# Softmax in eleven parts with halo rows from the neighbour, input loads on GpSimd's queue, z blocks in turn, another order of the value products

## The chip, the cores and the metric

One core of a Trainium2 chip runs the kernel. The metric is device time in microseconds of one execution; the median of three runs before the change is 603.17 us (594.58 to 603.51).

## The reference, cut to what matters

Sizes: B = 8 batches, S = 4224 rows, D = 192 channels, H = 8 heads of 24 channels, K = 7 taps, all float32.

```python
w = exp(weight_gen - max(weight_gen, axis=-1))          # (B, S, H, 7)
w = w / (sum(w, axis=-1) + 1e-9)                        # softmax over the 7 taps
out[b,s,h,:] = sum over k of w[b,s,h,k] * x[b, s-6+k, h,:]   # rows before 0 are zero
gate = sigmoid(sum over j of conv_w[j] * out[b, s-4+j, :])   # 5 taps, per channel
y = (gate * (out @ w_val)) @ w_out                      # two 192x192 products
```

## The kernel before, in words

**Softmax and z.** The softmax of weight_gen is computed in 7 parts of 192 to 960 sequence rows of each batch (R = 12, 16, 28, 28, 60, 60, 60 rows in each of 128 partitions; partition 16l+q holds rows q*R to q*R+R of batch l's part). Each part also holds the 6 rows behind each partition's own (`PAD`), loaded and computed a second time, because a z row needs the weights of later rows. On DVE: `max`, `sub`, `sum`, `recip`, `norm`; on ACT: `exp` (L224 to L250). Four ACT copies (`spread`, L267) then put the weights of up to 12 rows into a zero-filled tile `zt` (two of them), so that each row of 184 numbers is a piece of a banded matrix, and `store` (L281) writes it to a DRAM block z. Blocks are new and get whole rows with their zeros (736 B per row); the last part reuses the block of the fifth and writes only the 72 numbers that change (288 B per row).

**Groups.** The sequence is cut into 36 groups (the first and last of 72 rows, the others of 120), each for all 8 batches. For group m, `load_x` (L299) brings its rows and 6 before them into one of three tiles `xt`; `load_t` (L322) reads the banded matrix back out of z in some 8 pieces of 16 rows into one of two tiles `tb`. `bank` (L335) then does the dynamic convolution as matmuls, four kinds into PSUM tiles `pa` (three buffers). ACT's `evac` (L354) takes kinds 0 and 1 to `ringA`, kind 2 to `ringB`, kind 3 to a tile `S`; twelve small transfers on POOL's queue (`move`, L362 and L364, four to ringB, then eight to ringA) place the pieces of S into holes of the rings. The gate of a group is one ACT product (`tap0`, L382) and four DVE multiply-adds (`tap`, L389) for each of A and B, then a sigmoid on ACT (L394). `val` (L404 to L412) is the product with w_val, `gv` (L418, L420) the gating, `omm` (L433, L440) the product with w_out, `oev` (L454) its copy to `ot`, and `store` (L461) two transfers to the output, twice per group.

**Order.** Every call is put in a list with a hand-written time (`at`, `stage`) and the list is sorted: the times fix only the order on each engine and queue; waits are put in by data dependence. Group m's stage begins at `when(m)` (13.05 apart): its bank and moves fall in that stage, its taps and `val` in the next, `omm` in the one after that. `load_x` and `load_t` of group m stand at `when(m-1)`. All of weight_gen's loads (one for each batch and half part), x, z, tb and output transfers are issued by SP in that order, but for four on ACT; POOL issues the moves and, at the start, the weights' transfers, and fills tiles and converts the weights.

Of the kernel before, what the change touches and what calls it, by code (L numbers as in the profile page):

```python
# [17 lines left out]
def tile_dynconv_gated_moe(  # L18
# [47 lines left out]
    ZQ = 4  # L66
# [21 lines left out]
    wf = const.tile([P, 2, NWT], FP32, name="wf")  # L88
    un = const.tile([P, 2, NWT], U32, name="un")
# [4 lines left out]
    cw = wf[:, :, 2 * D:]  # L94
    woa = wf[:, 0, D:2 * D]
    wob = wf[:, 1, D:2 * D]
# [29 lines left out]
    def convert_weights(cs, v, w):  # L126

        lo_w, hi_w = raw[:, :, cs, 0], raw[:, :, cs, 1]
        t = wf[:, :, cs].bitcast(U32)
        u = un[:, :, cs]  # L130
        tf, uf = wf[:, :, cs], u.bitcast(FP32)
# [16 lines left out]
    def place_weights():  # L148
# [9 lines left out]
        pairs = [*runs(wvm, wf[:, 0, 0:D], 4, NQ)]  # L158
        for b in range(2):
            hs = slice(HD * b, HD * b + HD)  # L160
            pairs += runs(wvd[hs, hs], wf[hs, 1, 0:D], 4, NQ)
        pairs += [*runs(wva, wf[:, 0, 0:D], 0, 4), *runs(wvb, wf[:, 1, 0:D], 0, 4)]
# [9 lines left out]

    class Block:


        def __init__(self, n, name):
            self.n, self.used = n, False
            self.t = dpool.tile([L, n, PITCH], FP32, name=name)

    blocks = [Block(16 * R, f"z{i}") for i, R in enumerate((12, 16, 28, 28, 60, 60))]  # L180
# [3 lines left out]
    class Softmax:  # L184

        ROWS = 60 + PAD

        def __init__(self, r0, R, block):
            self.r0, self.R, self.n = r0, R, R + PAD
            self.block, self.old = block, block.used  # L190
            block.used = True
            assert block.n == 16 * R
            h = -(-self.n // 22)
            self.cut = [(self.n * k // h, self.n * (k + 1) // h) for k in range(h)]
            self.zc = [(c, min(c + ZR, R)) for c in range(0, R, ZR)]
            where.append(r0)

        def tiles(self):
            self.wt = wpool.tile([P, self.ROWS, H, K], FP32, name="wt")[:, 0:self.n]
            self.mx = wpool.tile([P, self.ROWS, H], FP32, name="mx")[:, 0:self.n]  # L200
            if self.r0 + 16 * self.R == S:
                nc.vector.memset(self.wt[P - Q:P, self.R:], 0.0)

        def load(self, l, c0, c1, eng):


            R = self.R
            flat = self.wt.rearrange("p r h k -> p (r h k)")
            src = wg.offset + (l * S + self.r0) * ROW

            def part(q, c0, c1):
                if c0 < c1:
                    s = bass.AP(tensor=wg.tensor, offset=src + c0 * ROW, ap=[[R * ROW, q], [1, (c1 - c0) * ROW]])
                    eng.dma_start(out=flat[16 * l:16 * l + q, c0 * ROW:c1 * ROW], in_=s)

            if l == L - 1 and self.r0 + 16 * R == S:
                part(16, c0, min(c1, R))
                part(15, max(c0, R), c1)
            else:
                part(16, c0, c1)  # L220

        def max(self, k):
            a, b = self.cut[k]
            nc.vector.tensor_reduce(out=self.mx[:, a:b], in_=self.wt[:, a:b], axis=AX.X, op=ALU.max)  # L224

        def wide(self, k):
            a, b = self.cut[k]
            return self.wt[:, a:b], self.mx[:, a:b].unsqueeze(3).broadcast_to([P, b - a, H, K])

        def sub(self, k):  # L230
            w, m = self.wide(k)
            nc.vector.tensor_tensor(out=w, in0=w, in1=m, op=ALU.subtract)

        def exp(self, k):
            a, b = self.cut[k]
            nc.scalar.activation(out=self.wt[:, a:b], in_=self.wt[:, a:b], func=AF.Exp)

        def sum(self, k):
            a, b = self.cut[k]
            nc.vector.tensor_reduce(out=self.mx[:, a:b], in_=self.wt[:, a:b], axis=AX.X, op=ALU.add)  # L240

        def recip(self, k):
            a, b = self.cut[k]
            m = self.mx[:, a:b]
# [3 lines left out]
        def norm(self, k):  # L248
            w, m = self.wide(k)
            nc.vector.tensor_tensor(out=w, in0=w, in1=m, op=ALU.mult)  # L250

        def spread(self, c):
# [5 lines left out]
            for e in range(2):  # L258
                for o in range(2):
# [7 lines left out]
                    nc.scalar.copy(out=dst, in_=src)  # L267

        def store(self, c):


            a, b = self.zc[c]
            d0 = self.block.t[0, a, :]
            step, n = (PITCH, DATA) if self.old else (ZQ * PITCH, ZQ * PITCH)
            dst = bass.AP(tensor=d0.tensor, offset=d0.offset,
                          ap=[[self.R * PITCH, P], [step, (b - a) * PITCH // step], [1, n]])
            if self.old:
                src = self.z[:, 0:b - a, 0:DATA]
            else:
                src = self.z[:, 0:b - a].rearrange("p (r q) c -> p r (q c)", q=ZQ)  # L280
            nc.sync.dma_start(out=dst, in_=src)  # L281


    class Group:
# [400 lines left out]
```

## Time and profile before

| | us |
|---|---|
| median of 3 runs | 603.17 (594.58 to 603.51) |
| the profiled execution | 596.75, span 595.0 |
| busy: PE / DVE / ACT / POOL | 489.3 / 422.0 / 316.8 / 257.8 |
| mean granted TensorE clock | 0.925 |
| moved by DMA | 115.44 MB |

Busy time is that of instructions on the engine; matmuls are pipelined, so a busy PE isn't at its peak. The granted clock is 1.0 at 2.4 GHz and 0.5 at 1.2 GHz. The DMA share is the mean busy share of the 16 DMA engines. A wait is put down to what came last by the profile.

### The profile page before, as it was taken

The numbers are of one execution on the slowest core, as the hardware profiler recorded it, in microseconds if no ns is written. First come the engines' busy times: TensorE is split into PE (matmuls) and PEld (weight loads), VectorE is DVE, ScalarE is ACT, GpSimd is POOL, SyncE is SP. The second block draws the span as 40 slices with busy tenths as digits, with TensorE's granted clock in tenths as the row PEclk, the third lists the DMA queues.
The fourth block names the chain that finished last, engine by engine and source line by source line (L and its number), as shares of the span: only waits on it lengthen the run. The fifth ranks groups of instructions, "written<-read, shape, count | busy, mean of one in ns | idle before, by whom it ended". The sixth has DMA issues, their size and how long they took to land.

```text
span 595.0 us, 15932 instructions
## 1 busy us (share of the span) xinstructions
PE 489.3 (82%) x6324; PEld 337.2 (57%) x6324; DVE 422.0 (71%) x470; ACT 316.8 (53%) x517; POOL 257.8 (43%) x465
## 2 busy tenths in 40 slices
PE   7056879887998179998978598899897999898895
PEld 4054546556665157764646465566566667576553
DVE  5928997957796648788876276786984674766681
ACT  7135683644965335855745334863864544544542
POOL 5675444424434144444442244444544544544440
PEclk9556998988999679998997799899998999999999
DMA  7599997998898988858999995749889777777422
GB/s 166 186 190 197 219 225 179 222 307 197 193 250 266 307 189 191 187 108 210 259 249 250 251 205 141 166 118 214 201 204 219 179 183 155 182 165 173 96 84 79
DMA packets 123415, 115.44 MB, mean 194 GB/s; under 512 B 31765, under 2 KB 118985, under 8 KB 121293
## 3 DMA queue, kind: packets, MB, share of 16 engines
q1 hardware_dynamic: 108637, 106.20, 72.8%
q0 software_dynamic: 14576, 7.97, 7.5%
q8 instruction: 50, 0.82, 0.7%
q10 hardware_dynamic: 128, 0.26, 0.2%
q14 instruction: 24, 0.20, 0.1%
HBM read 60.43 MB, written 47.98 MB: 182 GB/s over the span
## 4 chain that ended last, share of the span: by engine, by line
DMA 39%; issue 16%; PE 15%; POOL 10%; DVE 9%; ACT 6%; SPq 4%; ACTq 0%; DVEq 0%; POOLq 0%
DMA ringA<-S 11%; DMA ringB<-S 11%; POOL ringA L362 8%; DMA tb<-z 6%; DMA xt<-in_x_dram 6%; PE pa L335 6%; DVE aA L389 5%; PE po L433 4%; SPq L322 2%; DMA wt<-in_weight_gen_dram 2%; PE po L440 2%; DVE aB L389 2%; DMA out_dram<-ot 2%; POOL ringB L364 2%; DMA z<-zt 1%
## 5 line engine op out<-in xcount | busy, mean ns | idle before, releaser
L389 DVE SCALAR_TENSOR_TENSOR aA<-ringA,wf,aA 128x960 f32<-128x960 f32 (+1 forms) x144 | 171.4, 1190 | 97.4 <-ACT aA L382 75.5
L335 PE MATMUL pa<-tb,xt 126*32 126x120 f32 (+1 forms) x4608 | 150.9, 291 | 93.2 <-DMA tb<-z 36.7
L335 PEld LDWEIGHTS pa<-tb,xt 126*32 126x32 f32 (+1 forms) x4608 | 137.4, 120 | 106.5 <-issue 57.1
L362 POOL DMA_DIRECT2D ringA<-S x288 | 155.5, 547 | 93.5 <-ACT ringA L354 36.0
L364 POOL DMA_DIRECT2D ringB<-S x144 | 78.3, 549 | 209.3 <-ACT ringB L354 142.9
L389 DVE SCALAR_TENSOR_TENSOR aB<-ringB,wf,aB 128x480 f32<-128x480 f32 (+1 forms) x144 | 100.6, 699 | 30.9 <-ACT aB L382 27.9
L433 PE MATMUL po<-wf,aA 128*120 128x192 f32 (+1 forms) x576 | 109.6, 333 | 2.9 <-ACT ot L454 2.3
L433 PEld LDWEIGHTS po<-wf,aA 128*120 128x120 f32 (+1 forms) x576 | 93.4, 186 | 28.0 <-issue 20.4
L454 ACT COPY ot<-po 120x768 f32<-120x768 f32 (+1 forms) x72 | 57.6, 800 | 51.3 <-PE po L440 26.5
L440 PE MATMUL po<-wf,aB 64*120 64x192 f32 (+1 forms) x576 | 67.5, 353 | 1.8 <-ACT ot L454 1.8
L404 PE MATMUL v<-ringA,wva 128*128 128x480 f32 (+1 forms) x144 | 64.5, 568 | 2.1 <-DMA ringA<-S 2.1
L382 ACT ACTIVATE aA<-ringA,wf 128x960 f32<-128x960 f32 (+1 forms) x36 | 38.9, 1081 | 46.4 <-DMA ringB<-S 35.2
L394 ACT ACTIVATE aB<-aB 128x480 f32<-128x480 f32 (+1 forms) x36 | 21.5, 598 | 74.4 <-DVE aB L389 74.3
L440 PEld LDWEIGHTS po<-wf,aB 64*120 64x120 f32 (+1 forms) x576 | 45.6, 186 | 17.4 <-issue 13.1
L267 ACT COPY zt<-wt 128x192 f32<-128x192 f32 (+1 forms) x96 | 38.5, 480 | 18.0 <-DVE wt L250 9.9
L394 ACT ACTIVATE aA<-aA 128x960 f32<-128x960 f32 (+1 forms) x36 | 35.6, 990 | 19.8 <-DVE aA L389 19.8
L418 DVE TENSOR_TENSOR aA<-v,aA 128x960 f32<-128x960 f32 (+1 forms) x36 | 40.6, 1128 | 4.5 <-ACT aA L394 4.5
L354 ACT COPY S<-pa 128x480 f32<-128x480 f32 (+1 forms) x36 | 19.6, 544 | 42.8 <-PE pa L335 42.7
L407 PE MATMUL v<-ringB,wvb 64*128 64x480 f32 (+1 forms) x144 | 38.7, 614 | 0.0
L412 PE MATMUL v<-ringB,wvd 128*128 128x480 f32 (+1 forms) x72 | 38.0, 609 | 0.0
L354 ACT COPY ringA<-pa 128x480 f32<-128x480 f32 (+1 forms) x72 | 36.3, 545 | 2.0 <-PE pa L335 1.9
L404 PEld LDWEIGHTS v<-ringA,wva 128*128 128x128 f32 x144 | 26.5, 194 | 18.4 <-issue 17.6
(59 smaller groups left out, 335.3 us busy)
## 6 DMA issues: line engine op xcount, KB each, us to landing
xt<-in_x_dram SPq DMA_DIRECT2D x34, 756.0 KB
out_dram<-ot SPq DMA_DIRECT2D x136, 180.0 KB
tb<-z SPq DMA_DIRECT2D x205, 88.0 KB
z<-zt SPq DMA_DIRECT2D x16, 1104.0 KB
wt<-in_weight_gen_dram SPq DMA_DIRECT2D x79, 77.0 KB
ringA<-S POOLq DMA_DIRECT2D x272, 15.0 KB, 4.8
tb<-z SPq DMA_DIRECT2D x34, 64.0 KB
ringB<-S POOLq DMA_DIRECT2D x136, 15.0 KB, 4.6
```

Of the source, the lines that this page charges most:

```text
L335: nc.tensor.matmul(out=pa[Q * c:Q * c + Q, n * l:n * l + n], lhsT=self.xb[0:k, LH * u + l, C * h:C * h + Q], rhs=self.t[0:k, LH * u + l, P ...
L354: nc.scalar.copy(out=dst, in_=pa)
L362: nc.gpsimd.dma_start(out=ringA[q:q + h, LH * u:LH * u + LH, p0:p0 + n], in_=self.S[p:p + h])
L364: nc.gpsimd.dma_start(out=ringB[HD * u + q:HD * u + q + h, :, p0:p0 + n], in_=self.S[p:p + h])
L382: nc.scalar.activation(out=self.lanes(self.acc(g)), in_=self.src(g, 0), func=AF.Copy, scale=cw[:, g, 0:1])
L389: nc.vector.scalar_tensor_tensor(out=a, in0=self.src(g, j), scalar=cw[:, g, j:j + 1], in1=a, op0=ALU.mult, op1=ALU.add)
L394: nc.scalar.activation(out=a, in_=a, func=AF.Sigmoid)
L404: nc.tensor.matmul(out=v01[:, u, 0:w], lhsT=wva, rhs=A[u], start=True, stop=False)
L418: nc.vector.tensor_tensor(out=a, in0=self.v01[:, :, 0:w], in1=a, op=ALU.mult)
L433: nc.tensor.matmul(out=po[0:n, u, D * t:D * t + D], lhsT=gA[:, u, k, t], rhs=woa, start=first and t == 0, stop=not first, skip_group_check ...
L440: nc.tensor.matmul(out=po[0:n, u, D * t:D * t + D], lhsT=gB[hs, k, t], rhs=wob[hs], start=first and t == 0, stop=not first, skip_group_che ...
L454: nc.scalar.copy(out=self.ot[0:n], in_=self.po[0:n, :, 0:2 * D])
```

## The change: what it does

- Eleven parts (R = 6, 8, 16, 28, six of 30, 26) in four buffers instead of two. Parts 0 to 2 still hold their 6 halo rows (now those before a partition's own). Parts 3 to 10 don't compute them: after `norm` of the last rows, `halo` copies the neighbouring partition's last 6 rows (127 partitions, 1344 B each), and `first`, planned 3 us later, gets those of each batch's first partition from the part before (8 partitions); both are on POOL's queue. The last 6 rows of the sequence are stored in a block of their own (`ztail`).
- weight_gen of all parts but the first is loaded by POOL's queue, one transfer for all batches and each half part.
- z blocks: parts 4 and 5 have one each, and parts 6 to 9 reuse them in turn, writing only 288 B per row; rows of a new block are written in one run per partition.
- `load_x` brings 128 rows instead of 126. `load_x` and `load_t` of group m stand at `when(m-2) + 3.9`, 9 us earlier than before.
- `evac` of kind 3 stands ahead of `tap0` of B (0.95 for 1.55, against 1.5 for 0.85). In `val`, v2 comes before the second half of v01; in `omm`, the B part always comes first.
- At the start, other engines clear other pieces of the tiles, and the converted weights lie in three tiles. The planned stage is 12.9.

```diff
+    SIZES = (6, 8, 16, 28, 30, 30, 30, 30, 30, 30, 26)
...
-    for i, R in enumerate((12, 16, 28, 28, 60, 60, 60)):
-        parts.append(Softmax(r0, R, blocks[i if i < 6 else 4]))
+    for i, R in enumerate(SIZES):
+        same = [b for b in blocks if b.R == R]
+        if len(same) < 2:
+            same.append(Block(R, f"z{i}"))
+            blocks.append(same[-1])
+        b = same[0] if len(same) > 1 and i > 5 and i % 2 == 0 else same[-1]
+        parts.append(Softmax(i, r0, R, b))
...
+        def load(self, k, eng):
+            w = self.wt.rearrange("p r h k -> p (r h k)")
...
+            a, b = self.cut[k]
+            if self.i:
+                src = bass.AP(tensor=wg.tensor, offset=wg.offset + (self.r0 - PAD + a) * ROW,
+                              ap=[[S * ROW, L], [self.R * ROW, 16], [1, (b - a) * ROW]])
+                eng.dma_start(out=w[:, a * ROW:b * ROW], in_=src)
...
+        def halo(self):
+            w = self.wt.rearrange("p r h k -> p (r h k)")
+            nc.gpsimd.dma_start(out=w[1:P, 0:PAD * ROW], in_=w[0:P - 1, self.R * ROW:(self.R + PAD) * ROW])
+
+        def first(self):
+            v = parts[self.i - 1]
+            w, u = (t.wt.rearrange("p r h k -> p (r h k)") for t in (self, v))
+            nc.gpsimd.dma_start(out=w[0::16, 0:PAD * ROW], in_=u[15::16, v.R * ROW:(v.R + PAD) * ROW])
...
         def load_x(self):
             lo = max(0, PAD - self.s)
-            src = bass.AP(tensor=x.tensor, offset=x.offset + (self.s - PAD + lo) * D,
-                          ap=[[D, self.k - lo], [S * D, L], [1, D]])
-            nc.sync.dma_start(out=self.xb[lo:self.k, :, 0:D], in_=src)
+            n = self.n if lo else min(P, S - self.s + PAD)
+            n += 8 if lo else 0
+            for a, b in ((0, n),) if n % 16 == 0 else ((0, n // 16 * 16), (n // 16 * 16, n)):
...
             for u in range(2):
                 nc.tensor.matmul(out=v01[:, u, 0:w], lhsT=wva, rhs=A[u], start=True, stop=False)
+            nc.tensor.matmul(out=v2[:, 0:w], lhsT=wvd, rhs=Bt, start=True, stop=True)
+            for u in range(2):
+                nc.tensor.matmul(out=v2[HD * u:HD * u + HD, 0:w], lhsT=wvm, rhs=A[u], start=False, stop=True,
+                                 tile_position=(0, HD * u), skip_group_check=True)
             for u in range(2):
                 hs = slice(HD * u, HD * u + HD)
                 nc.tensor.matmul(out=v01[:, u, 0:w], lhsT=wvb[hs], rhs=Bt[hs], start=False, stop=True,
                                  tile_position=(HD * u, 0))
-            for u in range(2):
-                nc.tensor.matmul(out=v2[HD * u:HD * u + HD, 0:w], lhsT=wvm, rhs=A[u], start=True, stop=False,
-                                 tile_position=(0, HD * u))
-            nc.tensor.matmul(out=v2[:, 0:w], lhsT=wvd, rhs=Bt, start=False, stop=True)
...
-            if k == 0:
-                b_part(True)
-                a_part(False)
-            else:
-                a_part(True)
-                b_part(False)
+            b_part(True)
+            a_part(False)
...
-    T0, T1, TG = 21.0, 8.0, 13.05
+    T0, T1, TG = 17.0, 6.0, 12.9
...
-    at(0.4, load_all, parts[1], (nc.sync,))
+    at(0.035, load_all, parts[1], nc.gpsimd)
+    at(0.07, load_all, parts[2], nc.gpsimd)
...
+        if fn == s.norm:
+            if k == 0:
+                s.haloed = t
+                if not s.alone:
+                    at(t + 0.01, s.halo)
+                    s.haloed = t + 3.0
+                    at(s.haloed, s.first)
...
+        t = max(begin - 20.0, parts[i - 3].haloed + 0.03, parts[i - 4].ready + 0.03)
+        at(t, s.tiles)
+        for k in range(len(s.cut)):
+            at(t + 0.1 + 3.0 * k, s.load, k, nc.gpsimd)
...
-        if m >= 2:
-            stage(m - 1, 0.0, g.load_x)
+        if m >= 3:
+            stage(m - 1, -9.0, g.load_x)
         for i, j, lo, hi in g.segments():
-            t = max(when(m - 1) + 0.01 if m > 1 else 0.0, parts[i].ready + 0.01 * (m + 1))
+            t = max(when(m - 2) + 3.9 if m > 1 else 0.0, parts[min(i, len(parts) - 1)].ready + 0.01 * (m + 1))
...
-            stage(m, (1.55, 2.1, 3.75, 4.3)[i], g.evac, kind)
+            stage(m, (0.95, 2.1, 3.75, 4.3)[i], g.evac, kind)
...
-        stage(m + 1, 0.85, g.tap0, 1)
+        stage(m + 1, 1.5, g.tap0, 1)
```

## Rows read from the trace of the kernel before

**Rows 1.** The page, part 1: busy us and share of the span.
```profile
span 595.0 us, 15932 instructions
PE 489.3 (82%) x6324; PEld 337.2 (57%) x6324; DVE 422.0 (71%) x470; ACT 316.8 (53%) x517; POOL 257.8 (43%) x465
```

**Rows 2.** PE's timeline: start us, us, then the instructions; first rows of groups' banks.
```profile
31.41 4.07 PE L335 MATMUL pa<-tb,xt 78*32 78x72 f32 x128 [19.14 <-DMA tb<-z]
...
56.72 1.56 PE L335 MATMUL pa<-tb,xt 126*32 126x120 f32 x47
...
211.73 1.63 PE L335 MATMUL pa<-tb,xt 126*32 126x120 f32 x28 [15.87 <-DMA tb<-z]
...
494.10 3.67 PE L335 MATMUL pa<-tb,xt 126*32 126x120 f32 x128
...
506.76 2.84 PE L335 MATMUL pa<-tb,xt 126*32 126x120 f32 x96
...
562.67 1.81 PE L335 MATMUL pa<-tb,xt 78*32 78x72 f32 x96
```

**Rows 3.** Table by stretch: length, busy us of each engine, granted clock, DMA share, GB/s.
```profile
57.00:447.00 390.00, 330.97 (x4332) 228.23 (x4321) 296.37 (x323) 223.59 (x368) 160.56 (x297) 0.94 0.87 211
447.00:540.00 93.00, 85.74 (x1196) 60.37 (x1196) 56.90 (x64) 44.56 (x70) 41.69 (x78) 0.98 0.81 182
540.00:595.00 55.00, 45.42 (x472) 29.85 (x468) 32.21 (x39) 23.23 (x37) 18.84 (x35) 1.00 0.40 99
...
182.00:217.00 35.00, 17.50 (x270) 12.90 (x264) 16.67 (x19) 12.49 (x24) 8.95 (x17) 0.76 1.01 277
```

**Rows 4.** Waits over the span: who waited for what, us in total, times, longest.
```profile
PE pa L335 <- DMA tb<-z: 36.7, 4, 19.1
...
PE pa L335 <- ACT S L354: 27.7, 15, 7.5
...
SPq L322 <- DMA xt<-in_x_dram: 100.4, 30, 5.2
...
ACT aA L382 <- DMA ringB<-S: 35.2, 9, 5.4
...
POOL ringA L362 <- DMA ringB<-S: 31.6, 12, 4.5
...
DVE aB L420 <- PE v L412: 3.4, 4, 1.6
```

**Rows 5.** Timeline of the start.
```profile
15.14 1.44 DVE L224 TENSOR_REDUCE mx<-wt 128x176 f32<-128x1232 f32 x1 [4.13 <-DMA wt<-in_weight_gen_dram]
...
18.88 1.37 POOL L482 MEMSET tb<- 128x1472 f32 x1
...
22.74 0.36 SPq L281 DMA_DIRECT2D z<-zt  x1
...
34.30 2.33 POOL L364 DMA_DIRECT2D ringB<-S  x4 [2.62 <-ACT ringB L354]
...
47.94 0.52 ACT L382 ACTIVATE aB<-ringB,wf 128x288 f32<-128x288 f32 x1
```

**Rows 6.** DMA issues: engine and operation, count, KB each, median us to landing.
```profile
z<-zt SPq DMA_DIRECT2D x16, 1104.0 KB
ringA<-S POOLq DMA_DIRECT2D x272, 15.0 KB, 4.8
...
z<-zt SPq DMA_DIRECT2D x5, 432.0 KB
...
z<-zt SPq DMA_DIRECT2D x3, 368.0 KB
...
raw<-wd POOLq DMA_DIRECT2D x1, 384.0 KB, 3.3
```

**Rows 7.** Groups of instructions: busy us, mean ns of one, idle before them.
```profile
L362 POOL DMA_DIRECT2D ringA<-S x288 | 155.5, 547 | 93.5 <-ACT ringA L354 36.0 <-DMA ringB<-S 31.6 <-ACT aA L394 10.3
...
L224 DVE TENSOR_REDUCE mx<-wt 128x176 f32<-128x1232 f32 (+2 forms) x15 | 20.0, 1331 | 16.9 <-DMA wt<-in_weight_gen_dram 15.5 <-DMA tb<-z 1.3
```

More of the change, by code (lines that the diff above doesn't have):

```diff
@@ L222, in max @@
-        def max(self, k):
[L223 to L228, printed above, removed]
+            assert block.R == R
+            h = -(-R // 16)
+            c = [PAD + R - R * k // h for k in range(h + 1)]
+            self.alone = i < 3
+            if self.alone:
+                c[h] = 0
@@ L543, in tile_dynconv_gated_moe @@
+    for k, w in ((2, "DVE"), (0, "POOL"), (1, "POOL")):
+        for i, (eng, f) in enumerate(convert_weights(k, "DVE", w)):
+            t = (16.9, 22.0, 16.85)[k] + 0.005 * i if i < 7 else (21.5, 31.0, 16.89)[k]
             at(t, lambda f=f, eng=eng: f(engs[eng]))
     for i, f in enumerate(place_weights()):
[L545 to L554 removed]
+        at(22.0 + 0.05 * i, f)
@@ L580, in tile_dynconv_gated_moe, with z @@
+    at(1.25, load_all, parts[3], nc.gpsimd)
     JOB = (2.3, 10.4, 13.6)
-    EXP, SPREAD = 7.05, (5.0, 7.1, 11.5)
-    per = {m: 3 if m < 11 else 2 for m in range(2, NM + 2)}
-    begins = {3: 2, 4: 5, 5: 10, 6: 18}
+    EXP, SPREAD = 7.05, (5.0, 7.1)
     taken = set()
-    m, left = 2, per[2]
-    for i in range(3, len(parts)):
+    def z(t):
+        p, o = min((p, o) for p in range(1, NM) for o in SPREAD if (p, o) not in taken and when(p) + o > t)
+        taken.add((p, o))
+        return when(p) + o
@@ new lines, in tile_dynconv_gated_moe @@
+    order = [(0, 0), (1, 0), (0, 1), (2, 0), (1, 1), (2, 1), (3, 0), (3, 1)]
+    t = 4.5
+    for i, half in order:
+        s = parts[i]
+        for fn, k in jobs(s)[half]:
+            place(s, fn, k, t, z if i == 3 else lambda t: t + 0.02)
+            t += 0.06 * (s.cut[k][1] - s.cut[k][0]) + 0.15
+        if half == 0:
+            for k in range(len(s.cut)):
+                at(t, s.exp, k)
+    at(parts[1].ready + 0.005, gr[1].load_x)
+    at(parts[2].ready + 0.05, gr[2].load_x)
+    begin = 33.0
@@ L587, in tile_dynconv_gated_moe @@
+    slots = [(m, o) for m in range(1, NM) for o in JOB if (m, o) >= (1, 10.0)]
+    for i in range(4, len(parts)):
         s = parts[i]
         f, g = jobs(s)
-        if m < begins[i]:
-            m, left = begins[i], per[begins[i]]
-        if i > 3:
-            at(when(m - 2) + 4.0, s.tiles)
-            for c, (a, b) in enumerate(s.cut):
-                for l in range(L):
-                    at(when(m - 2 + c) + 4.1 + 0.5 * l, s.load, l, a, b, nc.sync)
-        else:
-            at(when(m - 1) + 6.0, load_all, s, (nc.sync,))
@@ new lines, in tile_dynconv_gated_moe @@
+        at(t, s.tiles)
+        for k in range(len(s.cut)):
+            at(t + 0.1 + 3.0 * k, s.load, k, nc.gpsimd)
+        m = 0
+        for fn, k in f:
+            m, o = slots.pop(0)
+            place(s, fn, k, when(m) + o, None)
+        e = m if when(m) + o < when(m) + EXP else m + 1
+        for j in range(len(s.cut)):
+            at(when(e) + EXP + 0.1 * j, s.exp, j)
+        taken.add((e, SPREAD[1]))
+        while when(slots[0][0]) + slots[0][1] < when(e) + EXP + 2.0:
+            slots.pop(0)
@@ L623, in stage @@
+        for fn, k in g:
+            m, o = slots.pop(0)
+            place(s, fn, k, when(m) + o, z)
+        begin = when(slots[0][0]) + slots[0][1]
     def stage(m, off, fn, *args):
```

259 lines of the change are left out of this document (108 added, 151 removed).

## The prediction

> **What bounds the kernel now.** I read the busy times first: PE is busy for 82% of the span, DVE for 71%, POOL for 43% [rows 1], so no engine is full. Then PE's timeline, taking the first matmul of each group's bank as its mark. Where nothing is late, one group follows the next after 506.76 - 494.10 = 12.66 us; but from group 2 (56.72) to group 35 (562.67) the mean is 505.95 / 33 = 15.33 us, from group 30 to 35 it is 13.7, and from group 2 to group 30, while softmax and z still run, 15.6 [rows 2]. So some 2.7 us per group are lost, and some 55 us go by before group 2. The table by stretch says to what: from 57 to 447 us the DMA engines are busy for 0.87 of the time, and in the worst stall, 182 to 217 us, for 1.01 of it, at 277 GB/s, with PE busy for half [rows 3]. There a bank waits 15.87 us for tb [rows 2], and the mean granted clock is 0.76 of the 2.4 GHz. The list of waits names the late parties: PE for tb (36.7 us) and for the copy of S (27.7 us); SP, itself waiting 100.4 us for x to land before it can issue further pieces of tb; ACT for the moves (35.2 us) [rows 4]. The bound is thus bursts of transfers that meet a look-ahead of one group, on a DMA system that is nearly full.
>
> **The change, part by part.**
>
> *Look-ahead.* x and tb of a group are issued 9 us earlier. Before, a load issued at `when(m-1)` had 13 us; now it has 22, as long as tb of group m-2 has been used, which is what it then waits for on SP. Queued behind that wait are the output and z stores; `ot` has four buffers and a z chunk is planned 20 us ahead of the load that reads it, so I cost this at nothing. The price if that cover fails is a spread that finds its `zt` still in flight: ACT then stands still for up to the 8.67 us that z and tb took together at the start (22.74 to 31.41 [rows 2, 5]). The gain: of PE's 36.7 us on tb the first 19.14 lie in the start [rows 2, 4]; the other 17.6, and the half-clock stretches after them, can go. What is late next is the DMA system's throughput.
>
> *Bytes.* z before: 16 x 1104 + 5 x 432 + 3 x 368 = 20,928 KB [rows 6]. After: 144 rows of new blocks at 92 KB (1104 / 12) and 120 reused rows at 36 (432 / 12) give 17,570 KB, 16% less. weight_gen: 264 + 3 x 6 = 282 rows for 306, 8% less. The halos add eight transfers of 127 x 1344 B, 1.4 MB in all. DMA work per group, as share times time: without softmax 0.81 x 13.7 = 11.1 us, with it 0.87 x 15.6 = 13.6 [rows 2, 3]; so softmax and z cost 2.5 us per group, and after the change about 0.85 x 2.5 + 0.2 = 2.3: 13.4 us per group. This is more than the 12.66 of the engines, so DMA becomes the plain bound while softmax runs. Taken to a share of 0.96 (between the 0.87 of now and the 1.01 of the full stretch) a group takes 14.0 us.
>
> *Softmax on DVE.* Five passes over 306 rows, one costing 20.0 us [rows 7], become passes over 282: 8% of some 100 us, 8 us of DVE time that is not on the path. Nothing.
>
> *S before tap0.* PE's 27.7 us on S arise because the copy of S queues on ACT behind a tap0 that waits for moves. Now it goes first, and tap0 of B is later by one copy. I take half of the 27.7 as gone, and it is within the 14.0.
>
> *val and omm in another order.* The same matmuls; v2 comes earlier and the second half of v01 later. DVE now waits 3.4 us in all for v2 [rows 4]: at best these go, at worst the product with v01 waits as much. Nothing.
>
> *Blocks in turn.* A store to part 4's block must wait for the loads that read it. They are planned over 40 us earlier. Nothing.
>
> *POOL's queue.* SP loses its loads of weight_gen, which are not what it waits for; POOL gains 18 larger ones, eight halos, eight `first`, at 0.55 us each [rows 7] to perhaps 1: 19 to 34 us on an engine that idles 57%. What counts is the order. POOL waits for earlier landings when transfers pile up (31.6 us [rows 4]): a move to ringA waits for one to ringB, so as I read it the ninth transfer waits for the first. In each of seven stages from part 4 on (groups 4, 8, ... 24, and 28 without a load), a halo stands before the moves to ringB, and half a part's load before those to ringA; the third move to ringA comes eight transfers after the halo, the last one eight after the load. A 384 KB transfer on a quiet POOL queue landed in 3.3 us, a small move on a busy one in 4.8 [rows 6]; a load of 430 KB is so priced between 3.3 and, with its bytes at the 211 GB/s of [rows 3] shared with an equal stream, 4 + 4 = 8 us. The moves need 4.4 us to reach their wait, so each stage pays 0 to 4 us, in seven 0 to 28. `first` waits for its halo and is issued after the moves. I take 1 us each, 7 us.
>
> *The start.* DVE stood 4.13 us for part 1's load, until 15.14, before part 0's `sum`; the first z store was issued at 22.74, the first matmul at 31.41 [rows 2, 5]. With 12 rows for 18, half of the clearing gone from DVE, and part 1 loaded from time 0, the first matmul should come near 21. But the first moves, at 34.30, can't come much earlier: POOL now clears 6.8 thousand more numbers per partition (1472 take 1.37 us [rows 5], so 6.3 us) and issues six loads ahead of them (3.3 us or more). They come between 30 and 37; I take 33.5. From there 2.3 us of issue and 4.8 of landing lead to the first tap0 at 40 to 41 for 47.94: group 2 starts some 8 us earlier, at 49. If POOL isn't late it is 42, if it is later 55.
>
> **The sum,** against the profiled execution of 596.75 us: 49 to group 2, 28 x 14.0 = 392 to group 30, 5 x 13.5 = 67 to group 35, 7 for POOL's queue, less what the 14.0 already holds of such waits (say all of it), and 34 from 562.67 to the end as before: 542. The median of the runs lies 6.4 us above the profiled execution; I add half, **545 us**. With 13.3 and 14.7 for the 14.0 and 42 to 55 for the start it is 518 to 571.
>
> **The rivals.**
>
> *Compute alone binds* (0.06): if transfers spread evenly take less than their present times, 33 x 13.0 + 47 + 34 = 510. For it: 12.66 occurs. Against: shares above 0.9 wherever z is stored [rows 3].
>
> *DMA stays as it is* (0.11): the loads are asked for earlier but SP still stands on x's landing (100.4 us [rows 4]) and the same bytes need the same time. Then only the start gains: 590 to 600. Against: the share is 0.87, not 1, and 0.81 after 447 us.
>
> *The moves loop* (0.13): x and tb are now issued at the very time of the moves to ringA, which then take the 7 us or so of a busy stretch instead of 4.8; tap0 of A waits, and the copies to the rings behind it on ACT, and so the next moves. With 1.2 us more per group and 2 us for each of the seven stages: 545 + 40 = 580.
>
> *The halo is slow* (0.11, the slower side): place, POOL's queue ahead of the moves. If its 127 partitions are not spread over the DMA engines but go through one, 171 KB pass at 211 / 0.87 / 16 = 15 GB/s: 11 us alone, 22 in turn with SP's stream. The third move to ringA, 3 us after the halo, waits for it: 8 to 19 us in each of eight parts, 64 to 150 us, since taps and copies hang on the moves. With 11 us each it is 545 + 88 = 633. It decides from about 6 us of delay per part (48 us, no gain left). For it: nothing in the trace has 127 partitions. Against: the transfers of POOL's queue shown here landed in 3.3 and 4.8 us [rows 6], the larger of 384 KB.
>
> The Trainium skill has a rule for this (DMA: Bandwidth & Descriptors, section Why a DMA increments its semaphore by 16 and not by 1): a transfer runs on the largest number of engines up to 16 that divides the outermost sizes, so 127 partitions run on one; it adds a measured exception by which some direct copies on GpSimd's queue still use all 16. By the rule the sum would be the 633, by the exception the 545; no run here shows which. The same rule gives x's 126 rows 14 engines and the new 128 rows all 16, a gain the sum leaves out.
>
> **How the numbers follow.** Forecast 0.59, with 518 to 571 as its own range; the rivals 0.06, 0.11, 0.13, 0.11. About 2% either way (591 and 615) is what a measurement of this kernel can tell from no change. Faster by more than that: forecast, compute, the moves loop, 0.78; same: 0.11; slower: 0.11. The range leaves out the halo, most of the unchanged case and the lowest of the compute case: 512 to 588.
>
> **What would show it.** Right: no wait of PE on tb above 5 us after group 2, a DMA share of 0.93 or more while softmax runs, groups 13.5 to 14.5 apart, the first matmul near 21 but group 2 near 49. Wrong: moves of POOL waiting for a halo's landing (the halo is slow), ACT's tap0 waiting longer than 35 us on the moves (the loop), PE still stopped on tb (DMA as it is), or a share below 0.85 with groups at 13 (compute binds).

## The result, and the profile after

The median went from 598.88 us (594.50 to 603.51, four runs) to **556.13 us** (550.84 to 561.50, four runs): a ratio of 0.928, with a 95% interval of 0.913 to 0.943. The forecast was 545, with a range of 512 to 588. The profiled execution below is the longest of the four, 561.5 us with a span of 559.7; it lies over 1.5% above the shortest, and the ratios here and below leave such slow runs out, while the medians and the rows of this profile do not.

The page's first part of the kernel after, of its busy times; every line number from here on is that of the kernel after:

```profile
PE 479.7 (86%) x6324; PEld 332.4 (59%) x6324; DVE 414.1 (74%) x493; ACT 323.2 (58%) x548; POOL 282.5 (50%) x504
```

The engines do the same work as before [rows 1]; POOL has 25 us more of it, in new transfers and clearing. PE's timeline, first rows of groups' banks (start, us, instructions), for groups 0, 1, 2, 3, 28, 29, 30 and 35:

```profile
33.05 4.07 PE L368 MATMUL pa<-tb,xt 78*32 78x72 f32 x128 [21.07 <-DMA tb<-z]
45.68 6.38 PE L368 MATMUL pa<-tb,xt 126*32 126x120 f32 x128 [8.56 <-DMA z<-zt]
56.18 2.84 PE L368 MATMUL pa<-tb,xt 126*32 126x120 f32 x96
...
82.36 3.69 PE L368 MATMUL pa<-tb,xt 126*32 126x120 f32 x128
...
432.42 3.66 PE L368 MATMUL pa<-tb,xt 126*32 126x120 f32 x125
...
454.00 3.71 PE L368 MATMUL pa<-tb,xt 126*32 126x120 f32 x128
466.51 3.68 PE L368 MATMUL pa<-tb,xt 126*32 126x120 f32 x128
...
528.91 2.36 PE L368 MATMUL pa<-tb,xt 78*32 78x72 f32 x128
```

Group 3 starts at 82.36 and group 35 at 528.91: 446.55 / 32 = 13.95 us each, for 15.33 before [rows 2]. But hardly any group takes 13.95. Most take 12.5, as 454.00 to 466.51 does, and about one in four takes 14 to 22: from group 5 to 6 it is 20.0, from 9 to 10 19.6, from 13 to 14 20.1, from 17 to 18 18.1, from 20 to 21 16.3, from 28 to 29 21.6. What these take above 12.5 adds up to 446.55 - 32 x 12.5 = **46.6 us**; I call it the excess, and it is the measure for the experiments. All of it lies before group 30.

The table by stretch (length, busy us of PE, PEld, DVE, ACT, POOL, granted clock, DMA share, GB/s):

```profile
47.00:437.00 390.00, 353.63 (x4771) 243.73 (x4764) 304.15 (x360) 242.39 (x404) 194.64 (x355) 0.94 0.88 212
454.00:528.00 74.00, 74.00 (x1040) 52.64 (x1040) 53.30 (x61) 44.29 (x76) 39.29 (x73) 1.00 0.81 207
90.00:437.00 347.00, 322.70 (x4328) 221.28 (x4327) 275.10 (x322) 219.68 (x364) 171.66 (x317) 0.96 0.89 214
```

From 454 to 528 PE is busy for all of the 74 us: 12.5 us is what PE itself needs for a group at a granted clock of 1.00 (2.4 GHz). While softmax runs the DMA share is 0.88 or 0.89, hardly above the 0.87 of before [rows 3].

The waits over the span (who waited for what, us in total, times, longest):

```profile
POOL wt L240 <- DVE wt L276: 47.5, 8, 7.4
ACT aA L415 <- DMA ringB<-S: 40.4, 7, 8.6
...
POOL ringA L395 <- DMA wt<-in_weight_gen_dram: 23.5, 7, 6.6
PE pa L368 <- DMA tb<-z: 21.1, 1, 21.1
...
PE pa L368 <- ACT S L387: 13.4, 6, 11.1
...
ACT zt L293 <- DMA wt<-wt: 10.3, 1, 10.3
```

PE's wait on tb is left at the start alone, and that on S has halved [rows 4]; of its 13.4 us 11.1 lie at 70.11 us, still in the start, and 2.3 after it. New are POOL's waits: 47.5 us in which the halo (L240) waits for the last step of norm (L276), and 23.5 us of moves to ringA that wait for a load of weight_gen. ACT still waits 40.4 us for moves to ringB. SP's own list has `SPq L355 <- DMA xt<-in_x_dram` at 71.4 us in 21 waits, for 100.4 in 30 before, and `SPq L355 <- DMA z<-zt` at 67.8 us in 15 waits, for 10.2 in 6 before: SP now stands nearly as long for z to land as for x.

DMA issues of the kernel after (count, KB each, median us to landing):

```profile
wt<-in_weight_gen_dram POOLq DMA_DIRECT2D x12, 420.0 KB, 8.1
ringA<-S POOLq DMA_DIRECT2D x272, 15.0 KB, 5.1
...
wt<-wt POOLq DMA_DIRECT2D x8, 166.7 KB, 5.8
...
wt<-wt POOLq DMA_DIRECT2D x8, 10.5 KB, 4.5
```

The 166.7 KB rows are the halos, the 10.5 KB rows `first`.

What a long group looks like, from group 5 to group 6, rows of POOL, ACT and PE:

```profile
99.42 0.56 POOL L240 DMA_DIRECT2D wt<-wt  x1 [7.43 <-DVE wt L276]
100.03 2.22 POOL L397 DMA_DIRECT2D ringB<-S  x4
102.24 0.61 POOL L230 DMA_DIRECT2D wt<-in_weight_gen_dram  x1
102.84 1.08 POOL L395 DMA_DIRECT2D ringA<-S  x2
107.77 1.24 POOL L395 DMA_DIRECT2D ringA<-S  x2 [3.85 <-DMA wt<-wt]
...
112.37 0.54 POOL L395 DMA_DIRECT2D ringA<-S  x1 [1.17 <-DMA wt<-in_weight_gen_dram]
...
114.07 1.10 POOL L397 DMA_DIRECT2D ringB<-S  x2
...
119.62 1.09 ACT L415 ACTIVATE aA<-ringA,wf 128x960 f32<-128x960 f32 x1 [8.57 <-DMA ringB<-S]
...
107.33 3.63 PE L368 MATMUL pa<-tb,xt 126*32 126x120 f32 x128
...
127.28 3.64 PE L368 MATMUL pa<-tb,xt 126*32 126x120 f32 x128
```

POOL stands 7.43 us in front of the halo, and the moves to ringB queue behind it. As the prediction read it, a ninth transfer waits for the first: the third move to ringA waits 3.85 us for the halo to land, and the last one 1.17 for the load. The next group's moves to ringB leave at 114 to 117 us, ACT waits 8.57 us for their landing, and PE's next bank comes 19.95 us after the last, 7.5 us late. The eight halos are issued at 56.65, 99.42, 156.54, 215.94, 272.27, 329.21, 382.91 and 437.14 us, and the five waits of over 6 us in front of ACT's tap0 of A end within 21 us of one of them.

The start:

```profile
18.08 1.44 DVE L255 TENSOR_REDUCE mx<-wt 128x176 f32<-128x1232 f32 x1 [2.06 <-DMA wt<-in_weight_gen_dram]
...
17.18 0.37 SPq L308 DMA_DIRECT2D z<-zt  x1
24.27 0.66 POOL L230 DMA_DIRECT2D wt<-in_weight_gen_dram  x1
25.07 2.99 SPq L355 DMA_DIRECT2D tb<-z  x7
...
36.60 2.23 POOL L397 DMA_DIRECT2D ringB<-S  x4
...
65.84 1.45 ACT L293 COPY zt<-wt 128x160 f32<-128x160 f32 x4 [10.31 <-DMA wt<-wt]
```

The first z store left 5.6 us earlier than before [rows 5], but its pieces of tb could be issued only 7.9 us later, and the first matmul came 8.0 us after that: 33.05, for 31.41 before. Then ACT stood 10.31 us for `first` of part 3, and group 3, which came at about 72.2 before, came at 82.36.

### The profile page after: what moved, and what is told of

Read it like the earlier page. It is cut to its first block, busy times and chain, and to the rows that moved or that the text cites. A ratio compares the mean times of both kernels' runs of the same rounds, so it can differ in the third digit from the quotient of the medians.

```text
span 559.7 us, 15917 instructions
## 1 busy us (share of the span) xinstructions
PE 479.7 (86%) x6324; PEld 332.4 (59%) x6324; DVE 414.1 (74%) x493; ACT 323.2 (58%) x548; POOL 282.5 (50%) x504
## 3 DMA queue, kind: packets, MB, share of 16 engines
q1 hardware_dynamic: 113685, 95.12, 67.7%
q0 software_dynamic: 17936, 17.17, 14.4%
## 4 chain that ended last, share of the span: by engine, by line
DMA 35%; PE 29%; issue 15%; POOL 12%; ACT 3%; SPq 2%; DVE 2%; ACTq 0%; POOLq 0%
DMA ringA<-S 8%; PE po L466 8%; DMA wt<-in_weight_gen_dram 8%; PE pa L368 7%; DMA ringB<-S 7%; POOL ringA L395 6%; DMA tb<-z 5%; PE po L473 4%; DMA xt<-in_x_dram 4%; PE v L437 4%; POOL ringB L397 3%; PE v L444 2%; DMA wt<-wt 2%; PE v L440 2%; PE v L438 2%
## 5 line engine op out<-in xcount | busy, mean ns | idle before, releaser
L422 DVE SCALAR_TENSOR_TENSOR aA<-ringA,wf,aA 128x960 f32<-128x960 f32 (+1 forms) x144 | 171.4, 1190 | 78.4 <-ACT aA L415 54.9
L368 PE MATMUL pa<-tb,xt 126*32 126x120 f32 (+1 forms) x4608 | 137.0, 275 | 49.3 <-DMA tb<-z 21.1
L368 PEld LDWEIGHTS pa<-tb,xt 126*32 126x32 f32 (+1 forms) x4608 | 125.5, 112 | 59.9 <-issue 21.4
L466 PE MATMUL po<-wf,aA 128*120 128x192 f32 (+1 forms) x576 | 115.5, 344 | 1.9 <-issue 1.9
L437 PE MATMUL v<-ringA,wva 128*128 128x480 f32 (+1 forms) x144 | 70.0, 603 | 18.9 <-DMA ringA<-S 14.1
L415 ACT ACTIVATE aA<-ringA,wf 128x960 f32<-128x960 f32 (+1 forms) x36 | 38.9, 1080 | 73.0 <-DMA ringB<-S 40.4
L473 PE MATMUL po<-wf,aB 64*120 64x192 f32 (+1 forms) x576 | 64.2, 342 | 4.0 <-ACT ot L483 4.0
L473 PEld LDWEIGHTS po<-wf,aB 64*120 64x120 f32 (+1 forms) x576 | 48.1, 186 | 26.9 <-issue 16.8
L293 ACT COPY zt<-wt 128x160 f32<-128x160 f32 (+2 forms) x116 | 41.2, 437 | 16.7 <-DMA wt<-wt 10.3
L427 ACT ACTIVATE aA<-aA 128x960 f32<-128x960 f32 (+1 forms) x36 | 35.8, 995 | 14.7 <-DVE aA L422 14.6
L440 PE MATMUL v<-ringA,wvm 128*64 128x480 f32 (+1 forms) x144 | 38.0, 608 | 0.0
```

Source lines behind the costliest of these rows:

```text
L368: nc.tensor.matmul(out=pa[Q * c:Q * c + Q, n * l:n * l + n], lhsT=self.xb[0:k, LH * u + l, C * h:C * h + Q], rhs=self.t[0:k, LH * u + l, P ...
L422: nc.vector.scalar_tensor_tensor(out=a, in0=self.src(g, j), scalar=cw[:, g, j:j + 1], in1=a, op0=ALU.mult, op1=ALU.add)
L427: nc.scalar.activation(out=a, in_=a, func=AF.Sigmoid)
L437: nc.tensor.matmul(out=v01[:, u, 0:w], lhsT=wva, rhs=A[u], start=True, stop=False)
L440: nc.tensor.matmul(out=v2[HD * u:HD * u + HD, 0:w], lhsT=wvm, rhs=A[u], start=False, stop=True, tile_position=(0, HD * u), skip_group_chec ...
L466: nc.tensor.matmul(out=po[0:n, u, D * t:D * t + D], lhsT=gA[:, u, k, t], rhs=woa, start=first and t == 0, stop=not first, skip_group_check ...
```

## The experiments

I began with two theories of the 46.6 us. **Order**: halo, `first` and loads stand in POOL's queue in front of moves and wait, or make them wait. **Load**: the moves land late because the DMA system is full, whatever their order. The ratios below are to the kernel before on the same chip, with 95% intervals, from up to four runs each (after: 0.928 [0.913, 0.943]). Excess is counted from group 3 to group 35 in the one profiled execution of each kernel, as above; kernels whose ratios can't be told apart show 36.4 to 52.5, so a difference of some 10 us in it says little. Each diff is against the kernel after.

**Order, all three moved**

```diff
-                    at(t + 0.01, s.halo)
-                    s.haloed = t + 3.0
+                    at(t + 2.6, s.halo)
+                    s.haloed = t + 5.6
...
-            at(t + 0.1 + 3.0 * k, s.load, k, nc.gpsimd)
+            at(t + (6.8 if i == 4 else 1.65) + 0.3 * k, s.load, k, nc.gpsimd)
```

> On POOL's queue the halo, both loads of the next part and the first-partition transfer stand behind all twelve moves of their stage instead of among them. Theory A (order on POOL's queue: the halo waits for norm ahead of the moves to ringB, and moves to ringA wait for the landings of halo and load): the eight long groups of the changed kernel, 44 us above 12.5 in sum, go to 13 or so, and the first spread of part 3 no longer waits 10.3 us at the start: 510 to 520 us, ratio to before about 0.86. Theory B (bursts of z stores and loads on the DMA engines make the moves late wherever they stand): under 10 us of gain, 546 or more, ratio 0.91 or more.

Measured: 564.33 us, ratio 0.935 [0.932, 0.938]; long groups of 20.2 to 22.9 us remain in its profiled execution (570.41 us). The halo's wait for norm is gone from the list of waits, but others have come (waits, then rows of POOL and ACT, of this run):

```profile
ACT zt L293 <- DMA wt<-wt: 34.0, 7, 7.6
POOL wt L247 <- DMA wt<-wt: 27.9, 6, 9.6
```

```profile
108.52 0.56 POOL L240 DMA_DIRECT2D wt<-wt  x1 [0.38 <-DVE mx L271]
109.07 1.21 POOL L230 DMA_DIRECT2D wt<-in_weight_gen_dram  x2
113.23 0.53 POOL L247 DMA_DIRECT2D wt<-wt  x1 [2.95 <-DMA wt<-wt]
...
122.03 1.45 ACT L293 COPY zt<-wt 128x160 f32<-128x160 f32 x4 [8.92 <-issue]
```

`first` (L247) waits on POOL for the halo, and is issued behind the loads; the spread that needs it stands on ACT for 8.92 us with everything queued behind it. (The profile names no releaser for this wait; `first` landed 8.74 us after its issue, at 121.97, just before the spread began.) The wait was moved, not removed.

**Order, halo and `first` alone**

```diff
-                    at(t + 0.01, s.halo)
-                    s.haloed = t + 3.0
+                    at(t + 2.6, s.halo)
+                    s.haloed = t + 5.6
```

> Only the halo and the first-partition transfer stand behind the stage's moves; the loads stay among them. Theory A: POOL's 47.5 us of waits for norm and 9.2 for the halo's landing no longer hold moves, its 23.5 us for the loads' landing stay: 530 to 540 us. Theory B: as before the edit, 546 to 560.

Measured: 574.09 us, 0.944 [0.936, 0.953], long groups of 19.6 to 25.7. ACT's spreads wait 30.8 us for `first`: the same new wait.

**Order, loads alone**

```diff
-            at(t + 0.1 + 3.0 * k, s.load, k, nc.gpsimd)
+            at(t + (6.8 if i == 4 else 1.65) + 0.3 * k, s.load, k, nc.gpsimd)
```

> Only the loads of the next part stand behind the stage's moves; the halo stays ahead of them. Theory A: the 23.5 us of waits of moves for the loads' landing go, the waits for norm and halo stay: 535 to 545 us. Theory B: as before the edit, 546 to 560.

Measured: 563.44 us, 0.934 [0.929, 0.939], long groups of 16.3 to 21.3. The halo waits for norm as before (45.7 us), moves to ringA wait 28.5 us for the loads that now come in a pair, and ACT's spreads 36.5 us for `first`.

**Loads on SP's queue**

```diff
-            at(t + 0.1 + 3.0 * k, s.load, k, nc.gpsimd)
+            at(t + 0.1 + 3.0 * k, s.load, k, nc.sync)
```

> The changed kernel with the loads of parts 4 to 10 on SP's queue again, in the same large pieces and at the same planned times. If POOL's queue is what they cost, the moves no longer wait for their landing and nothing else moves: 535 to 545 us, as with the loads behind the moves. If SP's queue is the tighter one (its pieces of tb wait for earlier landings), tb and z come late: 560 or more.

Measured: 578.80 us, 0.962 [0.956, 0.968]: some 20 us slower than after, and the intervals lie apart. SP now waits 27.3 us in 12 waits for loads to land before it issues pieces of tb, and often two groups in four are long (19.6 and 17.7, 14.5 and 19.1, 15.5 and 17.5, 14.4 and 20.6), not one.

**Loads on ACT's queue**

```diff
-            at(t + 0.1 + 3.0 * k, s.load, k, nc.gpsimd)
+            at(t + 0.1 + 3.0 * k, s.load, k, nc.scalar)
```

> The changed kernel with the loads of parts 4 to 10 on ACT's queue, in the same pieces at the same planned times. If the loads hurt because they share POOL's queue with the moves, and SP's with tb, a third queue frees both: the long groups lose the 3 to 4 us of waits for the loads' landing, 535 to 545 us. If what hurts is their bytes at that time (theory B), as the changed kernel: 550 to 560.

Measured: 568.45 us, 0.940 [0.936, 0.945], excess 57.5. POOL's queue has no load in it now, yet the loss is no smaller (the intervals of the two ratios overlap). SP's own waits of this run show the place: pieces of tb (L355) wait 29.1 us and output stores (L490) 28.2 us, in 13 waits, for the landing of loads that ACT issued, and PE waits on tb 42.1 us in 7 waits: 31.1 in the first two, in the start, and late in the run one of 5.06 and one of 3.22. By the medians GpSimd's is the best of the three queues for the loads; against SP's that is clear, against ACT's not.

**Order, with `first` far later**

```diff
-                    s.haloed = t + 3.0
+                    s.haloed = t + (5.9 if s.i == 3 else 17.8)
```

> The changed kernel with only the first-partition transfer moved behind the two spreads that don't need it; halo and loads stand among the moves as in the change. Theory C: the start gains the 10.3 us of part 3's spread, the long groups stay near 18 to 20 us, since moves still wait for halo and loads: 540 to 550 us. Theory B: 550 to 560.

Measured: 552.60 us, 0.915 [0.911, 0.919], excess 41.4, group 3 at 77.64. With `first` out of the way of ACT's spreads this trace is 4.7 us shorter at the start and 5.2 in the long groups; the intervals of the two ratios overlap.

**Order, everything behind what it delayed**

```diff
-                    at(t + 0.01, s.halo)
-                    s.haloed = t + 3.0
+                    at(t + 2.6, s.halo)
+                    s.haloed = t + (5.9 if s.i == 3 else 17.8)
...
-            at(t + 0.1 + 3.0 * k, s.load, k, nc.gpsimd)
+            at(t + (6.8 + 5.9 * k if i == 4 else 1.65 + TG * k), s.load, k, nc.gpsimd)
```

> The halo and one load stand behind the moves of their stage, the second load behind those of the next stage, and the first-partition transfer comes after the two spreads that don't need it. Theory C (in the earlier runs the long group only changed its cause: ACT's spread waits for the first-partition transfer, which waits for the halo and lies behind the loads on POOL's queue): with both causes gone the long groups of 18 to 22 us go to 13 or 14: 510 to 525 us, ratio 0.86. Theory B (bursts of z stores and loads on the DMA engines make some group late wherever things stand): 550 or more, ratio 0.92 or more.

Measured: 555.15 us, 0.911 [0.905, 0.916], excess 36.4, long groups of 15.1 to 17.5 for 16.3 to 21.6. The halo's wait for norm is gone from the list, and so is most of what `first` cost. But a new wait has come: `DVE mx L255 <- DMA wt<-in_weight_gen_dram` stands at 40.8 us in 10 waits, for 6.1 in 2 in the kernel after, since the later loads now come late for the softmax. And an excess 10 us lower is also what the kernel with tap0 before S shows, further down, which leaves POOL's order alone. So what the order by itself is worth can't be read from this run.

**A quarter of the bytes less, order as it is.** The loads of x are left out from group 6 on, so that later groups work on old rows.

```diff
-        if m >= 3:
+        if 3 <= m < 6:
             stage(m - 1, -9.0, g.load_x)
```

> The changed kernel without x's loads from group 6 on (its groups then compute with rows of earlier groups): 0.77 MB per group less, a quarter of all bytes, in the same order on every queue. Theory B (the transfers are too many, so their landings stretch and make a group late): moves, halo and loads land in 3 to 5 us, the long groups fall to 13 to 14, 510 to 520 us. Theory A (the order on POOL's queue itself): the halo still waits for norm ahead of the moves, and the ninth transfer for the first: the long groups stay at 17 or more, 540 or more.

Measured: 529.30 us, 0.885 [0.877, 0.893], excess **16.0**, long groups of 13.8 to 14.7. The window, waits, issues and the stage that corresponds to the one shown above:

```profile
90.00:437.00 347.00, 336.31 (x4594) 232.87 (x4596) 295.32 (x345) 234.52 (x394) 185.55 (x343) 1.00 0.78 175
```

```profile
POOL wt L240 <- DVE wt L276: 43.5, 8, 7.4
POOL ringA L395 <- DMA wt<-in_weight_gen_dram: 32.0, 13, 3.4
```

```profile
wt<-in_weight_gen_dram POOLq DMA_DIRECT2D x12, 420.0 KB, 7.9
ringA<-S POOLq DMA_DIRECT2D x272, 15.0 KB, 4.4
...
wt<-wt POOLq DMA_DIRECT2D x8, 166.7 KB, 3.2
...
wt<-wt POOLq DMA_DIRECT2D x8, 10.5 KB, 2.5
```

```profile
99.23 0.56 POOL L240 DMA_DIRECT2D wt<-wt  x1 [7.42 <-DVE wt L276]
...
113.47 1.09 ACT L415 ACTIVATE aA<-ringA,wf 128x960 f32<-128x960 f32 x1 [3.52 <-DMA wt<-wt]
```

The halo waits for norm as long as in the kernel after (7.42 and 7.43 us in this stage, 43.5 and 47.5 in all), and the moves wait even longer for loads. But the halo lands in 3.2 us for 5.8, `first` in 2.5 for 4.5 and a move in 4.4 for 5.1, and ACT's tap comes at 113.47, not 119.62. The same order costs a third of what it did. That is what the load theory says, with one reservation: without x, SP's waits shrink as well (2.5 us on x for 71.4, 40.7 on z for 67.8), so stores and pieces of tb are issued earlier, and this run can't separate that from the landings.

**x in 126 rows again**

```diff
-            for a, b in ((0, n),) if n % 16 == 0 else ((0, n // 16 * 16), (n // 16 * 16, n)):
...
-                nc.sync.dma_start(out=self.xb[lo + a:lo + b, :, 0:D], in_=src)
+            src = bass.AP(tensor=x.tensor, offset=x.offset + (self.s - PAD + lo) * D,
+                          ap=[[D, self.k - lo], [S * D, L], [1, D]])
+            nc.sync.dma_start(out=self.xb[lo:self.k, :, 0:D], in_=src)
```

> The changed kernel with x's 126 rows in one transfer as before the change, for 128. If the row count sets how many DMA engines share the work (14 for 126), x lands later and some engines carry more: 8 to 15 us slower than the changed kernel, 564 to 571, ratio 0.94. If it doesn't matter: 551 to 560.

Measured: 567.46 us, 0.948 [0.936, 0.959], excess 53.8. Some 11 us slower than after by the medians; the two intervals overlap from 0.936 to 0.943. SP's wait on x is not longer than in after (70.9 us in 21 waits, for 71.4), so where these 11 us would arise isn't shown.

**The look-ahead undone**

```diff
-            stage(m - 1, -9.0, g.load_x)
+            stage(m - 1, 0.0, g.load_x)
...
-            t = max(when(m - 2) + 3.9 if m > 1 else 0.0, ...)
+            t = max(when(m - 1) + 0.01 if m > 1 else 0.0, ...)
```

> The changed kernel with load_x and load_t of a group again one stage ahead (9 us later). The look-ahead's worth by the prediction: the stalls of PE on tb return wherever z is stored, 1 to 1.5 us per group, 590 to 605 us, ratio 0.98 to 1.01. If the smaller parts and z pieces alone removed the stalls: 550 to 565, ratio 0.92 to 0.94.

Measured: 563.35 us, 0.933 [0.928, 0.937], excess 52.5: at most a few us, within the interval of after. The waits of PE on tb do not come back: the list has 27.6 us in two waits, both in the start, in front of the banks at 32.49 and 44.17 us. SP's waits change places: 115.3 us on x in 33 waits and 15.6 on z in 8, for 71.4 and 67.8 in after. Groups 30 to 35 take 67.7 us, for 62.4.

**tap0 before S again**

```diff
-            stage(m, (0.95, 2.1, 3.75, 4.3)[i], g.evac, kind)
+            stage(m, (1.55, 2.1, 3.75, 4.3)[i], g.evac, kind)
...
-        stage(m + 1, 1.5, g.tap0, 1)
+        stage(m + 1, 0.85, g.tap0, 1)
```

> The changed kernel with tap0 of B ahead of the copy of S on ACT again. The prediction gave this order no gain of its own beyond its groups of 14 us: then 551 to 562. If it is what removed PE's waits on S (27.7 us before, 13.4 after), a late move holds the copy of S and the next moves: 8 to 20 us slower, 564 to 576.

Measured: 553.92 us, 0.927 [0.917, 0.938], excess 36.4. No difference in time that can be told; PE waits 17.8 us on S, 10.4 of them in the start.

**The best order found**

```diff
-                    at(t + 0.01, s.halo)
-                    s.haloed = t + 3.0
+                    at(t + (0.01 if s.i == 3 else 2.6), s.halo)
+                    s.haloed = t + (5.9 if s.i == 3 else 17.8)
...
-    at(1.25, load_all, parts[3], nc.gpsimd)
+    at(1.75, load_all, parts[3], nc.gpsimd)
...
-            at(t + 0.1 + 3.0 * k, s.load, k, nc.gpsimd)
+            at(t + (0.1 + 3.0 * k if i == 4 else 1.65 + TG * k), s.load, k, nc.gpsimd)
```

> POOL's order as in the kernel with halo, loads and first-partition transfer behind the moves, but with the first steps of the change for parts 3 and 4, and part 3's loads issued behind the weights' transfers at the start. Theory B: the long groups near 15 to 17 remain, the start gains 3 to 5 us from the later loads: 542 to 548. If the start's loads don't hold z and tb of part 0: group 3 at 78 to 82 as before, 548 to 553.

Measured: **547.88 us** (545.75 to 549.10), 0.917 [0.906, 0.927]: 8 us below after by the medians (not run beside each other; the intervals overlap), and below the kernel before by 52.7 us. Its group 3 is at 72.79, where the kernel after has 82.36 and the other kernels 77.6 to 85.8: the start alone accounts for the 8 us. Its stretch that answers to that of after:

```profile
90.00:437.00 347.00, 319.75 (x4278) 221.60 (x4280) 274.27 (x321) 215.79 (x362) 176.48 (x325) 0.99 0.90 218
```

The halo's wait for norm has come down from 47.5 to 2.1 us, and the excess is still 40.4 us, at a DMA share of 0.90. Here too DVE now waits for loads, 31.2 us in 9 waits, and the longest of these, 8.13 us, lies in the longest group (20.8 us from 334.51): the mended order has a price of its own.

## Why the prediction was right in its time, and where its steps failed

The time and the direction came out as forecast, by a sum whose terms err in both directions; that they nearly cancel is luck. Against the profiled execution:

```
stretch               forecast   measured
to group 2              49        56.18
group 2 to 3            14.0      26.18
groups 3 to 30          378       384.15 (466.51 - 82.36; 14.23 each)
groups 30 to 35         67        62.40 (12.48 each)
to the end              34        30.79
sum                     542       559.70
```

**What the gain of 43 us comes from** is not what the prediction put it on. Undoing one step at a time costs some 20 us for the loads of parts 4 to 10 back on SP's queue, some 11 for x in 126 rows, a few for the look-ahead, and nothing for S before tap0; only the first of these is clear of the intervals. That first step stood in the prediction without a gain. The fewer bytes of z and weight_gen, the halo copies as such and the other steps were not undone by themselves.

**Bytes, and DMA as the plain bound: the number holds by luck, the mechanism fails.** I said that 13.4 us of DMA work per group would exceed the engines' 12.66 and make every group 14.0. The measured mean is 14.23, but 19 of these 27 groups take 12.4 to 13.2 us, most of them PE's own 12.5, while softmax is going on, and the share is 0.88, not the 0.93 or more that I named as the sign. DMA work per group with softmax, as share times time, is 0.88 x 14.23 = 12.5 us, not 13.4, and so no more than PE's own 12.5: it doesn't bound every group. A share taken in one kernel is not a fixed amount of work that one may carry into the next. What the load seems to do, by the run without x, is to stretch landings in the stages where POOL's queue leaves no slack.

**POOL's queue: the mis-sized term.** I took 7 us, with 0 to 28 as the bounds, and let the 14.0 swallow it; the long groups, nearly all in or right behind just these stages, cost most of the 46.6. Three things were left out. The halo waits on POOL for norm, 47.5 us in eight waits, with the moves to ringB behind it: I had looked at what waits for the halo's landing, not at what the halo itself waits for. A load lands in 8.1 us, at the upper end of my 3.3 to 8. And `first`, which I placed harmlessly behind the moves, holds ACT's spread (10.31 us once in the kernel after, 34.0 in seven when the loads go ahead of it). The runs don't split the 46.6 between order and load. With these waits mended 36.4 and 40.4 are left, but both kernels bring a new wait of DVE for loads (40.8 and 31.2 us), and the kernel with tap0 before S has 36.4 with POOL's order as it was; with lighter transfers and the order unmended 16.0 are left. So the long groups sit where POOL's queue is tight, and by the run without x the load sets most of the price; how much of the latter is the landings and how much SP's release from x stays open, and so does the price of the order itself. The stage without a load, from 432.42 to 454.00, says that a load in the queue isn't needed for a long one.

**Look-ahead: the wait went, but not by this step alone.** PE's tb waits after the start are gone, as forecast, but they stay gone with the look-ahead undone. What the step did is to exchange SP's wait on x (115.3 us undone, 71.4 with it) for one on z (15.6 undone, 67.8 with it): the cover of 20 us for z, which I costed at nothing, does not hold on SP's queue. PE's waits come back, in small (9.4 us in three waits of 1 us or more after the start), when the loads of weight_gen leave GpSimd's queue for ACT's. So the step that I waved away (SP loses loads "which are not what it waits for") is part of what cured them: on SP's or ACT's queue those loads hold up pieces of tb for 27.3 us or more. With x in 126 rows PE waits 3.9 us on tb, in three waits of the whole run. Smaller z pieces were not tried against this wait by themselves.

**x in 128 rows** I left out of the sum; it is worth some 11 us by the medians, with intervals that overlap. The Trainium skill (DMA: Bandwidth & Descriptors, section Why a DMA increments its semaphore by 16 and not by 1) gives 126 rows 14 engines and 128 rows 16; the direction of the medians agrees, the count of engines was not read here.

**S before tap0.** Half of PE's wait on S went (27.7 to 13.4 us), but mostly for another reason. After the start, 20.2 us of it became 2.3 (before, 7.5 of the 27.7 lie at 49.84 us); with the step undone it is 7.4. Undoing it costs no time that can be told: right as "within the 14.0". **Softmax on DVE, val and omm, blocks in turn** were costed at nothing, and none was undone by itself, so that isn't shown.

**The start** was forecast 7 us too early to group 2 and 19 to group 3, and the first matmul came at 33.05, not near 21. I took z and tb to land as quickly as before (8.67 us together); z took 7.9 us and tb 8.0. For tb the runs name the transfer: in all eight kernels that issue part 4's first load at 23.6 to 25.9 us (24.27 in the kernel after), the first matmul comes 7.9 to 9.1 us after the first piece of tb is issued; in the five that issue this load at 27.3 us or later, on whatever queue, 4.8 to 5.0. For z they point to part 3's loads: where these leave at 21 us, in the best order, z takes 4.7 us; in the others, where they leave at 9.4 to 12.8, 6.4 to 8.4. An earlier first matmul didn't bring an earlier group 2 by itself: it starts at 54.9 to 61.2 us in those five, and at 53.9 to 58.5 in the eight. Issuing part 3's loads and its `first` later gains 9.6 us to group 3. The first moves at 36.60 lie within the 30 to 37 that I gave, at its late end.

**The rivals.** *The slow halo* is false as the work of one engine: 166.7 KB landed in 5.8 us, and in 3.2 with fewer bytes about, where one engine at the 15 GB/s of the prediction would need 11. By the Trainium skill (DMA: Bandwidth & Descriptors, section Why a DMA increments its semaphore by 16 and not by 1) 127 partitions go through one engine, but for some direct copies on GpSimd's queue that use all 16: these times speak for the exception, though engines were not counted. The sign that I gave for this rival did come, in small: moves to ringA wait 9.2 us in four waits for a halo's landing. *DMA as it is* is false: groups fell from 15.6 to 14.2. *The moves loop* came in part: ACT's waits for moves to ringB grew from 35.2 to 40.4 us and moves to ringA land in 5.1 us for 4.8, but the long ones sit behind the halos, not in every group. (Its sum in the prediction doesn't come out: 28 x 1.2 + 7 x 2 is 47.6, which gives 593, not 580.) *Compute alone binds* is true of about half of the groups up to group 30, with 12.5 us, and of all of them after 454 us.

## What to carry to other kernels

Look at the distribution of group times before you price a mean: a mean of 14 made of 12.5 and 20 asks first in which stages the 20 arise and what stands in them, before it is taken for a steady bound. When a transfer is added to a queue, ask first what it waits for itself, since everything behind it waits as well; then what its landing admits. And a transfer whose wait has slack on a quiet system loses that slack on a busy one: test the order and the load apart, and look in each mended kernel for the wait that has taken the old one's place. And undo the steps that were priced at nothing, too: here the one with the largest effect was among them.

## What the runs showed of the hardware

The loads of 420 KB land in 8.1 us at a share of 0.89 and in 7.9 at 0.78, while the halos go from 5.8 to 3.2 and `first` from 4.5 to 2.5: between these two runs the traffic beside them hardly mattered to the large loads, and much to the others.

DVE's small tensor-scalar operation took many times its usual duration where POOL was clearing memory. Rows of DVE and POOL in the kernel after:

```profile
12.54 1.80 DVE L271 TENSOR_SCALAR mx<-mx 128x96 f32<-128x96 f32 x1
...
21.90 2.52 DVE L271 TENSOR_SCALAR mx<-mx 128x112 f32<-128x112 f32 x1
...
51.52 0.22 DVE L271 TENSOR_SCALAR mx<-mx 128x112 f32<-128x112 f32 x1
...
11.63 2.64 POOL L511 MEMSET tb<- 128x3024 f32 x1
...
21.69 0.73 POOL L551 MEMSET zt<- 128x736 f32 x1
...
23.00 1.35 POOL L511 MEMSET tb<- 128x1472 f32 x1
```

The one of 128x112 takes 0.22 us at 51.52, where POOL clears nothing. The two long ones end at 14.34 and 24.42, each 0.07 us after POOL's clearing ends (14.27 and 24.35): by these rows they waited for it, the second through three clearings in a row (from 21.69, 22.35 and 23.00). The reduction from 18.08 to 19.52 overlaps another clearing and takes its usual 1.44. The Trainium skill (SBUF — State Buffer, section SBUF: two separate sides) tells of a pair of ports that DVE's two-port operations and GpSimd's share, held by the one that starts first for its whole instruction while the other is blocked; the first of these rows agrees, and so does the second if the pair stayed with POOL from one clearing to the next. So the clearing that the change moved to POOL takes some 4 us from DVE at the start, which the prediction had not counted.
